# One fused attention and two-layer expert kernel: a new hand-written order for its first batch, and parts of the second batch's attention moved to later steps

## Chip, core and metric

The kernel runs on one core of one Trainium2 chip. The metric is the device time of one execution in microseconds (us). Of the kernel before, three runs are shown: 1402.45, 1406.14 and 1407.8 us, median 1406.14 us.

## What is computed

Three stages feed each other. Stage 1 is attention over a small memory: for each of 8 batches and 8 heads, `phi` (576 x 32) goes through a softmax and condenses `k` and `v` (576 x 64) into 32 memory rows; the queries attend to these 32 rows. Stage 2 takes the 4608 tokens with 512 features through two dense layers with an ELU between them. Stage 3 sends each token to one of 8 experts (the arg-max of a small product), through two more layers with a ReLU.

```python
a = softmax(phi); k_m = einsum('bhsm,bhsd->bhmd', a, k); v_m = einsum('bhsm,bhsd->bhmd', a, v)
x = softmax(q @ k_m.T / 8) @ v_m          # tokens x 512
g = elu(x @ w_in);  y = g @ w_out         # w_in 512 x 2048, w_out 2048 x 512, float64 in HBM
e = argmax(y @ w_gate);  out = gate * (relu(y @ w1[e]) @ w2[e])
```

## The kernel before

Stages 1 and 2 go batch by batch; the product of attention and the first layer is regrouped, so that a batch's `v_m` is first multiplied with `w_in` (names `M`, `n.M`) and the result, in `wt0`, is the stationary side of `mm1`. The unit of work is a step: `mm1` (6 matmuls, L509), `elu` (two ScalarE activations and one VectorE operation, L516 to L518), `split_g` (a ScalarE rounding L525 and a subtraction L526 on VectorE or GpSimd that gives high and low halves), `mm2` (12 matmuls, L541). A batch has 32 steps, two halves (g = 0, 1) of 16. Step numbers in this text count from the start: steps 0 to 31 are batch 0 (the half g = 1 is cut in two, so that its last 8 steps come at 24 to 31), step 32 is the first of batch 1. The matmuls of step i + 2 (`mm1`) are issued in loop turn i.

During the first batch the kernel also reads both weight matrices, which lie in HBM as 64-bit floats, and turns them into float32 halves by integer operations. For each of 16 loads n: `x.n` (DMA), `A0.n` (ScalarE, L264 and L269), `A1.n.r` (VectorE, L278, L281 and L284), `R.n.r` (GpSimd, L292). An even n is a slice of w_in, used by `M` and written to DRAM by `B.n`; an odd n is a slice of w_out, whose high half `C.n` (ScalarE, L308) makes and whose low half `D.n.r` (L320, 128 x 512) is made on VectorE where `LO_V` names (n, r), on TensorE where `LO_PE` does, else on GpSimd. `GL_V` likewise names the steps whose L526 is on VectorE. Slices 1, 6, 10 and 13 go in halves (r = 0, 1); for the others the names with r = 1 do nothing.

The attention of one batch comes in two halves u of four heads: `phi.u`, `kv.u`, `q.u` (loads), `a1`, `a1e` (softmax of phi), `a2` (transposes), `a3` (the sums over k and v, 48 records of L369, which wait for the kv load), `a3b`, `a4t`, `a4` (scores, L413), `a5`, `a5e`, `a5b`, `a5m` (softmax over 32), `a5c`, `a5d` (the operand of `mm1`, L458 on ScalarE and L459 on GpSimd). With `n.` in front they belong to batch 1. The kv tile has one buffer. In the first batch the same buffer holds the weight slices n >= 3 that are being converted (`conv_h`): they wait for `a3.1`, and the next `kv` load, `n.kv.0`, waits for the last of them.

The order of all this is written by hand: the string `START` is the order in which the named pieces are issued, and every engine and the DMA queue of SyncE works through its own share of it in that order. `LATER` puts further pieces in front of numbered loop turns from 23 on; from turn 24 on the framework orders instructions itself. Everything behind a waiting instruction on the same engine waits with it. `y_items` gives the turns, after a half-batch is finished, in which its tokens' expert is chosen, ranked and scattered.

```python
tag="kv"            # load_kv: one buffer, shared with conv_h["h"] for n >= 3
t = [1, 2, 4, 5, 6, 8, 10]   # y_items: logit, logit2, rank, first scatter, rows 0 to 2
```

Of the kernel before, what the change touches and what calls it, by code (L numbers as in the profile page):

```python
# [23 lines left out]


START = """
A1.5.1 phi.0 A1.12.1 kv.0 A1.9.1 a1.0 R.3.1 a1e.0 a2.0.0 phi.1 q.0 a2.0.1 routing x.3 a1.1 R.15.1 a1e.1 a3.0 a3b.0
a2.1.0 a4t.0 R.8.1 a2.1.1 kv.1 a4.0 a5.0 a3.1 x.2 R.0.1 A1.7.1 R.9.1 q.1 A0.3 A1.3.0 a5e.0 x.1 R.2.1 a5b.0 a5m.0
a3b.1 A0.2 a5c.0 R.11.1 R.3.0 a4t.1 x.0 A1.3.1 A1.2.0 a4.1 a5d.0 R.14.1 C.3 a5.1 A0.1 x.4 A1.1.0 R.2.0 A1.1.1 A0.0
a5e.1 D.3.1 A1.8.1 A1.0.0 A1.2.1 a5b.1 A0.4 R.7.1 A1.4.1 D.3.0 x.5 R.4.1 R.1.1 R.1.0 C.1 A1.4.0 R.0.0 a3c A0.5 a5m.1  # L30
a5c.1 D.1.0 A1.5.0 D.1.1 n.phi.0 R.4.0 a5d.1 M.0 R.5.1 Me.0 x.6 A0.6 M.1 B.0 n.a1.0 A1.6.0 B.4 Me.1 mm1.0 R.5.0 C.5
x.7 B.2 mm1.1 elu.0 M.2 elu.1 g.0 A1.11.1 mm1.2 x.8 mm1.3 A1.6.1 D.5.1 D.5.0 Me.2 g.1 R.6.0 elu.2 R.6.1 B.6 elu.3
A0.7 mm2.0 A1.7.0 g.2 x.9 g.3 mm2.1 M.3 mm1.4 A0.8 elu.4 mm1.5 mm2.2 Me.3 mm2.3 g.4 elu.5 R.7.0 A1.8.0 x.10 mm1.6
mm1.7 mm2.4 C.7 g.5 elu.6 elu.7 A0.9 D.7.0 n.phi.1 R.8.0 x.11 D.7.1 mm1.8 g.6 mm2.5 mm1.9 mm2.6 A1.9.0 R.12.1 g.7
elu.8 swap R.9.0 A1.15.1 mm2.7 A0.10 elu.9 mm1.10 g.8 part A1.10.0 A1.0.1 mm1.11 elu.10 elu.11 B.8 mm2.8 g.9 C.9
mm1.12 g.11 M.4 mm2.9 A1.10.1 mm1.13 D.9.1 g.10 elu.12 x.12 A0.11 mm1.14 D.9.0 mm2.10 A1.14.1 A1.11.0 mm2.11 Me.4
R.10.0 A0.12 elu.13 elu.14 g.13 R.10.1 R.11.0 g.12 M.5 A1.12.0 w.0 B.10 g.14 Me.5 mm1.15 mm1.16 mm2.12 C.11 R.12.0
x.13 elu.15 mm2.13 elu.16 D.11.1 A0.13 D.11.0 g.16 mm2.14 mm1.17 g.15 M.6 mm1.18 elu.17 A1.13.0 x.14 mm2.15 mm2.16
A0.14 A1.14.0 elu.18 x.15 mm1.19 g.17 Me.6 B.12 n.a1e.0 A1.13.1 g.18 A0.15 mm2.17 A1.15.0 mm1.20 n.a2.0 R.14.0 w.1
mm2.18 elu.19 M.7 elu.20 g.19 R.13.0 mm1.21 R.13.1 R.15.0 Me.7 g.20 mm2.19 B.14 C.13 D.13.0 D.13.1 elu.21 mm1.22  # L40
elu.22 g.21 C.15 g.22 n.a1.1 mm2.20 D.15.0 D.15.1 n.kv.0 n.q.1 n.a3.0 n.q.0 n.a1e.1 mm2.21 n.a3b.0 n.a4t.0 mm2.22
n.a2.1 n.a4t.1 n.a4.0 mm1.24 n.kv.1 n.a3.1 n.a5.0 mm1.23 elu.24 n.a3b.1 n.a5e.0 elu.23 g.24 g.23 n.a3c
"""
# [12 lines left out]

# [1226 lines left out]
```

## Time and profile before

| | |
|---|---|
| median of the three runs | 1406.14 us |
| the profiled execution | 1407.8 us |
| its span, first to last instruction | 1406.1 us |
| mean granted TensorE clock (1.00 is 2.4 GHz, 0.50 is 1.2 GHz) | 0.977 |
| busy: TensorE, its weight loads, VectorE, ScalarE, GpSimd | 93%, 80%, 44%, 45%, 31% |

PE is TensorE's matmuls, PEld its weight loads, DVE is VectorE, ACT is ScalarE, POOL is GpSimd, SP is SyncE, whose rows are DMA issues. A matmul's end is modelled, so neighbouring matmuls overlap in the rows; the distance of their starts is what one costs. In a timeline row the bracket is the idle time of the engine before the row and what ended it. The last letters of a matmul's name in the views are its operands: `ps_kv` is a3, `ps_s` a4, `ps_M` M, `ps_h` mm1, `ps_acc` mm2.

### The profile page before, as it was taken

The page shows a single profiled execution, that of the slowest core. Times are in us where ns is not written, and L with a number is a line of the kernel's source. Part 1 is how long each engine was busy: PE and PEld are TensorE (multiplying, and loading weights), DVE is VectorE, ACT ScalarE, POOL GpSimd, SP SyncE. Part 2 cuts the span into 40 slices and gives each one's busy share as a digit, 9 for nine tenths or more (in the row PEclk, how much of TensorE's full clock was granted, in tenths as well). Part 3 has the DMA queues.
Part 4 walks back from the last instruction along what each step waited for, and adds up shares of the span by engine and source line. Part 5 has one row for each costly group of instructions (what it writes and reads, how often), then busy time and mean ns, then how long its engine had stood idle before and what let it go on. Part 6 is the DMA issues. An engine that isn't in the chain of part 4 may idle for free. (4 is left out here: it accounts for less than half of the span.)

```text
span 1406.1 us, 27602 instructions
## 1 busy us (share of the span) xinstructions
PE 1304.9 (93%) x9407; PEld 1121.6 (80%) x9407; DVE 625.0 (44%) x1355; ACT 633.1 (45%) x1377; POOL 441.6 (31%) x480
## 2 busy tenths in 40 slices
PE   3498699999999999999899999999999999999996
PEld 2287588889889888799789889878888888888885
DVE  4998454343443534434433324553222555342221
ACT  3586255555565555555455556422111443231110
POOL 2665143334433433434334343221111111111111
PEclk9898799999999999999999999999999999999998
DMA  9765745235325333433421510054111444211110
GB/s 238 202 207 154 178 121 130 62 114 102 90 83 103 103 79 94 139 71 92 103 76 37 167 28 24 18 185 154 46 46 41 159 143 141 72 46 44 34 47 31
DMA packets 57626, 140.74 MB, mean 100 GB/s; under 512 B 9321, under 2 KB 21738, under 8 KB 53872
## 3 DMA queue, kind: packets, MB, share of 16 engines
q1 hardware_dynamic: 49328, 118.15, 30.5%
q0 software_dynamic: 8128, 20.50, 4.7%
q8 instruction: 85, 1.39, 0.5%
q14 instruction: 85, 0.70, 0.2%
HBM read 253.79 MB, written 24.02 MB: 198 GB/s over the span
## 5 line engine op out<-in xcount | busy, mean ns | idle before, releaser
L526 POOL TENSOR_TENSOR gl<-e,gh 128x288 fp32r<-128x288 f32 x243 | 198.7, 819 | 376.5 <-ACT gh L525 296.8
L541 PE MATMUL ps_acc<-gl,wt 128*128 128x288 f32 x1024 | 306.6, 299 | 6.3 <-DVE gl L526 3.6
L541 PE MATMUL ps_acc<-gh,wt 128*128 128x288 f32 x1024 | 305.7, 299 | 1.9 <-ACT gh L525 1.9
L541 PE MATMUL ps_acc<-gh,wol 128*128 128x288 f32 x1024 | 302.9, 296 | 0.0
L509 PE MATMUL ps_h<-ath,wt 128*128 128x288 f32 x1024 | 263.2, 313 | 10.0 <-DVE e L518 9.9
L509 PEld LDWEIGHTS ps_h<-ath,wt 128*128 128x128 f32 x1024 | 181.8, 192 | 50.2 <-issue 29.5
L518 DVE SCALAR_TENSOR_TENSOR e<-e,ps_h 128x288 f32<-128x288 f32 x256 | 114.7, 450 | 238.4 <-ACT e L517 201.8
L541 PEld LDWEIGHTS ps_acc<-gl,wt 128*128 128x128 f32 x1024 | 195.3, 191 | 12.5 <-DVE gl L526 6.4
L541 PEld LDWEIGHTS ps_acc<-gh,wt 128*128 128x128 f32 x1024 | 195.5, 191 | 2.9 <-ACT gh L525 2.5
L1109 PE MATMUL ps_h<-wt,xh 128*128 x592 | 196.2, 402 | 1.3 <-ACT xh L1090 0.8
L541 PEld LDWEIGHTS ps_acc<-gh,wol 128*128 128x128 f32 x1024 | 195.1, 191 | 0.0
L525 ACT CAST gh<-e 128x288 fp32r<-128x288 f32 x256 | 109.7, 430 | 153.0 <-DVE e L518 151.0
L1150 POOL DMA_INDIRECT out_dram<-ot,idw x37 | 37.1, 1004 | 390.4 <-DVE ot L1149 378.6
L509 PE MATMUL ps_h<-atl,wt 128*128 128x288 f32 x512 | 153.7, 300 | 0.0
L516 ACT ACTIVATE e<-ps_h 128x288 f32<-128x288 f32 x256 | 104.8, 410 | 82.3 <-PE ps_h L509 72.4
L1109 PEld LDWEIGHTS ps_h<-wt,xh 128*128 128x128 f32 x592 | 112.1, 189 | 27.2 <-ACT xh L1090 1.0
L1143 PE MATMUL ps_acc<-wt1h,hh 128*128 x296 | 120.9, 408 | 5.7 <-PEq L1187 5.7
L1125 ACT CAST hh<-ps_acc 128x512 fp32r<-128x512 f32 x74 | 39.8, 590 | 175.6 <-PE ps_acc L1123 175.5
L1143 PE MATMUL ps_acc<-wt1l,hh 128*128 x296 | 118.6, 401 | 0.0
L1109 PE MATMUL ps_h<-wt,xl 128*128 x296 | 117.9, 398 | 0.2 <-DVE xl L1091 0.2
L1143 PE MATMUL ps_acc<-wt1h,hl 128*128 x296 | 117.9, 398 | 0.0
L517 ACT ACTIVATE e<-e 128x288 f32<-128x288 f32 x256 | 113.8, 445 | 7.3
(242 smaller groups left out, 1829.3 us busy)
## 6 DMA issues: line engine op xcount, KB each, us to landing
raw<-in_moe_w_dram SPq DMA_DIRECT2D x78, 2048.0 KB
win<-win_s SPq DMA_DIRECT2D x28, 1024.0 KB
kv<-in_k_dram SPq DMA_DIRECT2D x16, 576.0 KB
kv<-in_v_dram SPq DMA_DIRECT2D x16, 576.0 KB
table<-yr SPq DMA_DIRECT2D x144, 64.0 KB
big<-in_moe_w_out_dram SPq DMA_DIRECT2D x10, 512.0 KB
phi_t<-in_phi_dram SPq DMA_DIRECT2D x16, 288.0 KB
big<-in_q_dram SPq DMA_DIRECT2D x16, 288.0 KB
```

What stands on the lines that cost most here:

```text
L509: nc.tensor.matmul(ps, x[:, u, fo:fo + P], y[:, u], start=(n == 0), stop=(n == 3 * NQ - 1))
L516: nc.scalar.activation(out=e, in_=ps, func=AF.Relu, scale=-1.0)
L517: nc.scalar.activation(out=e, in_=e, func=AF.Exp, scale=-1.0)
L518: nc.vector.scalar_tensor_tensor(out=e, in0=e, scalar=-1.0, in1=ps, op0=ALU.add, op1=ALU.max)
L525: nc.scalar.copy(out=gh, in_=e)
L526: eng.tensor_tensor(out=gl, in0=e, in1=gh.bitcast(F32), op=ALU.subtract)
L541: nc.tensor.matmul(acc[c], x[:, f, P * c:P * c + P], y, start=(first and n == 0), stop=(final and n == 2),)
L1109: nc.tensor.matmul(ps, x[:, c], half(wt[0][y][2 * c + hf]), start=(i == 0), stop=(i == 3 * NC - 1))
L1125: nc.scalar.copy(out=h, in_=ps)
L1143: nc.tensor.matmul(ps, get(h, f), half(wt[1][y][f]), start=(i == 0), stop=(i == 3 * NF2 - 1))
L1150: nc.gpsimd.indirect_dma_start(out=out, out_offset=IndirectOffsetOnAxis(ap=at, axis=0), in_=ot, in_offset=None, bounds_check=NT - 1, oob_i ...
```

## The change

Three things are replaced: the order of the first batch (`START`) and the two sets that place its subtractions; the turns in `LATER` of batch 1's attention; and the turns of the first half-batch's ranking. No operation is added or taken away. The two orders, their sets and the last line in full:

```diff
 START = """
-A1.5.1 phi.0 A1.12.1 kv.0 A1.9.1 a1.0 R.3.1 a1e.0 a2.0.0 phi.1 q.0 a2.0.1 routing x.3 a1.1 R.15.1 a1e.1 a3.0 a3b.0
-a2.1.0 a4t.0 R.8.1 a2.1.1 kv.1 a4.0 a5.0 a3.1 x.2 R.0.1 A1.7.1 R.9.1 q.1 A0.3 A1.3.0 a5e.0 x.1 R.2.1 a5b.0 a5m.0
-a3b.1 A0.2 a5c.0 R.11.1 R.3.0 a4t.1 x.0 A1.3.1 A1.2.0 a4.1 a5d.0 R.14.1 C.3 a5.1 A0.1 x.4 A1.1.0 R.2.0 A1.1.1 A0.0
-a5e.1 D.3.1 A1.8.1 A1.0.0 A1.2.1 a5b.1 A0.4 R.7.1 A1.4.1 D.3.0 x.5 R.4.1 R.1.1 R.1.0 C.1 A1.4.0 R.0.0 a3c A0.5 a5m.1
-a5c.1 D.1.0 A1.5.0 D.1.1 n.phi.0 R.4.0 a5d.1 M.0 R.5.1 Me.0 x.6 A0.6 M.1 B.0 n.a1.0 A1.6.0 B.4 Me.1 mm1.0 R.5.0 C.5
...
-mm2.18 elu.19 M.7 elu.20 g.19 R.13.0 mm1.21 R.13.1 R.15.0 Me.7 g.20 mm2.19 B.14 C.13 D.13.0 D.13.1 elu.21 mm1.22
-elu.22 g.21 C.15 g.22 n.a1.1 mm2.20 D.15.0 D.15.1 n.kv.0 n.q.1 n.a3.0 n.q.0 n.a1e.1 mm2.21 n.a3b.0 n.a4t.0 mm2.22
-n.a2.1 n.a4t.1 n.a4.0 mm1.24 n.kv.1 n.a3.1 n.a5.0 mm1.23 elu.24 n.a3b.1 n.a5e.0 elu.23 g.24 g.23 n.a3c
+routing phi.0 R.2.1 A1.9.1 x.1 kv.0 a1.0 A1.2.1 phi.1 a1e.0 A0.1 a2.0.0 R.7.1 a2.0.1 A1.1.0 A1.1.1 R.1.1 R.1.0 a3.0
+q.0 a1.1 a1e.1 a2.1.0 a3b.0 A1.8.1 R.5.1 a4t.0 x.2 kv.1 a2.1.1 A0.2 a4.0 C.1 q.1 a5.0 R.3.1 A1.7.1 x.3 A1.2.0 x.0
+a5e.0 a5b.0 D.1.1 D.1.0 a5m.0 a4t.1 a3.1 R.2.0 x.5 a5c.0 a3b.1 a4.1 a5d.0 A1.3.1 a5.1 A0.3 A1.3.0 a3c A0.0 a5e.1
+a5b.1 M.1 A1.0.0 R.3.0 R.0.1 A0.5 a5m.1 a5c.1 x.4 C.3 D.3.0 R.11.1 R.0.0 Me.1 A0.4 x.6 a5d.1 D.3.1 A1.4.0 B.2 M.0
+Me.0 R.4.1 A1.5.0 mm1.0 A0.6 elu.0 mm1.2 A1.6.0 R.14.1 elu.2 R.4.0 g.0 A1.4.1 M.2 Me.2 mm1.1 R.5.0 elu.1 R.12.1 C.5
...
+elu.18 g.16 A0.14 mm1.19 A1.14.0 R.13.1 mm2.16 g.18 elu.19 B.12 x.15 A0.15 n.q.0 mm1.20 A1.15.0 R.14.0 C.13 mm2.17
+mm2.18 g.19 w.0 elu.20 M.7 Me.7 mm1.21 elu.21 D.13.0 g.20 mm2.19 g.21 R.15.0 C.15 mm1.22 n.phi.1 D.13.1 mm2.20
+D.15.1 elu.22 D.15.0 B.14 mm2.21 g.22 n.q.1 n.kv.0 n.a4t.0 n.a1e.0 w.1 mm2.22 n.a2.0 n.a1.1 mm1.24 mm1.23 n.a4t.1
+elu.24 elu.23 g.24 g.23 n.a1e.1
 """
 LATER = {
-    23: "n.a5b.0 n.a5m.0 n.q2.0",
-    24: "n.M.0 n.a5c.0",
-    25: "n.pk2 n.a4.1 n.a5.1 n.a5e.1 n.a5b.1",
-    26: "n.q2.1",
-    27: "n.M.1",
-    29: "n.a5d.0",
-    30: "n.a5m.1 n.a5c.1 n.a5d.1",
-    31: "n.M.2",
-    35: "n.M.3",
+    24: "n.a3.0 n.a3b.0 n.kv.1 n.a2.1",
+    25: "n.a4.0 n.a5.0 n.a5e.0",
+    26: "n.a3.1 n.a3b.1 n.a5b.0 n.a5m.0 n.q2.0",
+    27: "n.pk2 n.a3c n.a4.1 n.a5.1 n.a5e.1 n.a5c.0",
+    28: "n.M.0 n.a5b.1 n.a5m.1 n.q2.1",
+    29: "n.a5d.0 n.a5c.1 n.a5d.1",
+    31: "n.M.1",
+    34: "n.M.2",
+    38: "n.M.3",
 }
-            LO_V = {(5, 0), (7, 1), (9, 1), (11, 0), (11, 1), (13, 0), (15, 0)}
+            LO_V = {(3, 0), (5, 1), (13, 1), (15, 0), (15, 1)}
-            GL_V = {0, 3, 4, 6, 12, 13, 14, 16, 18, 19, 21, 23, 24}
+            GL_V = {0, 1, 2, 4, 5, 6, 7, 8, 10, 11, 12, 14, 17, 19, 20, 21, 22, 23, 24}
-                t = [1, 2, 4, 5, 6, 8, 10] if g else [1, 2, 4, 5, 6, 8, 10]
+                t = [1, 2, 6, 7, 6, 8, 10] if b == 0 and g == 0 else [1, 2, 4, 5, 6, 8, 10]
```

## Rows read from the trace of the kernel before

**Rows 1.** Busy time by stretch: stretch, its length, PE, PEld, DVE, ACT, POOL, clock, DMA

```profile
0.00:200.00 200.00, 134.76 (x1110) 108.40 (x1111) 145.20 (x249) 107.87 (x211) 90.58 (x78) 0.88 0.69 185
200.00:400.00 200.00, 194.44 (x1756) 173.48 (x1754) 87.38 (x224) 112.69 (x265) 77.39 (x91) 1.00 0.41 105
```

**Rows 2.** The same view, in finer stretches of the first 198 us

```profile
0.00:26.00 26.00, 10.75 (x140) 7.58 (x140) 8.56 (x22) 6.24 (x11) 3.67 (x16) 1.00 0.93 230
26.00:62.00 36.00, 10.02 (x58) 3.79 (x58) 34.54 (x42) 21.58 (x32) 22.50 (x15) 0.95 0.76 201
62.00:125.00 63.00, 57.60 (x448) 50.32 (x448) 60.38 (x86) 51.73 (x103) 39.01 (x24) 0.95 0.73 214
125.00:141.00 16.00, 11.35 (x63) 9.61 (x63) 11.78 (x19) 7.68 (x17) 8.31 (x6) 0.66 0.29 98
141.00:150.00 9.00, 0.26 (x8) 0.29 (x12) 0.00 (x0) 0.06 (x2) 0.75 (x1) 0.50 0.86 200
150.00:198.00 48.00, 42.79 (x386) 34.81 (x379) 29.92 (x81) 19.29 (x46) 15.54 (x17) 0.81 0.50 141
```

**Rows 3.** Timeline of VectorE: start, duration, engine, line, operation, tiles

```profile
26.57 0.69 DVE L278 TENSOR_SCALAR conv_h<-conv_h 128x1024 f32<-128x1024 f32 x1 [5.86 <-ACT conv_h L264]
27.29 0.69 DVE L281 TENSOR_SCALAR conv_h<-conv_h 128x1024 uint32<-128x1024 uint32 x1
28.02 1.23 DVE L284 SCALAR_TENSOR_TENSOR conv_h<-big,conv_h 128x1024 uint32<-128x1024 uint32 x1
...
130.09 2.09 DVE L526 TENSOR_TENSOR gl<-e,gh 128x288 fp32r<-128x288 f32 x1
...
138.01 0.45 DVE L526 TENSOR_TENSOR gl<-e,gh 128x288 fp32r<-128x288 f32 x1
```

**Rows 4.** Timeline of GpSimd

```profile
20.89 1.16 POOL L428 TENSOR_TENSOR sT<-sT,mx 128x576 f32<-128x576 f32 x1 [17.46 <-DVE mx L423]
...
129.44 2.42 POOL L292 TENSOR_TENSOR conv_h<-conv_h,big 128x1024 uint32<-128x1024 uint32 x1 [2.76 <-DVE conv_h L284]
...
140.03 1.71 POOL L320 TENSOR_TENSOR wol<-conv_h,wt 128x512 fp32r<-128x512 f32 x1
...
185.23 1.55 POOL L459 TENSOR_TENSOR atl<-atT,ath 128x288 fp32r<-128x288 f32 x2 [0.59 <-ACT ath L458]
```

**Rows 5.** Groups by line, 0 to 152 us, VectorE: count, busy us, mean ns

```profile
L320 DVE TENSOR_TENSOR wol<-conv_h,wt 128x512 fp32r<-128x512 f32 x7 | 9.8, 1408 | 0.0
L526 DVE TENSOR_TENSOR gl<-e,gh 128x288 fp32r<-128x288 f32 x11 | 9.2, 844 | 0.2
```

**Rows 6.** The same view of GpSimd

```profile
L526 POOL TENSOR_TENSOR gl<-e,gh 128x288 fp32r<-128x288 f32 x12 | 12.2, 1022 | 14.6 <-ACT gh L525 14.6
L320 POOL TENSOR_TENSOR wol<-conv_h,wt 128x512 fp32r<-128x512 f32 x5 | 8.1, 1628 | 1.2 <-ACT wt L308 1.2
```

**Rows 7.** Timeline of TensorE

```profile
62.31 1.43 PE L471 MATMUL ps_M<-t,vT 64*32 64x256 f32 x16 [8.40 <-DVE wt L481]
63.67 0.61 PE L509 MATMUL ps_h<-ath,wt 128*128 128x288 f32 x1
...
149.74 2.79 PE L369 MATMUL ps_kv<-kv,a 96*32 96x128 f32 x48 [11.27 <-DMA kv<-in_v_dram]
...
160.00 1.52 PE L369 MATMUL ps_kv<-kv,a 96*32 96x128 f32 x48
...
197.94 0.30 PE L509 MATMUL ps_h<-ath,wt 128*128 128x288 f32 x1
198.08 0.30 PE L509 MATMUL ps_h<-atl,wt 128*128 128x288 f32 x1
```

**Rows 8.** Timeline of SyncE's DMA issues

```profile
141.78 0.34 SPq L196 DMA_DIRECT2D kv<-in_k_dram  x1
...
152.58 0.33 SPq L196 DMA_DIRECT2D kv<-in_k_dram  x1
```

**Rows 9.** Timeline of ScalarE

```profile
25.41 1.12 ACT L264 ACTIVATE conv_h<-big 128x1024 f32<-128x1024 f32 x1 [9.24 <-PE ps_kv L369]
```

More of the change, by code (lines that the diff above doesn't have):

```diff
@@ L32 @@
[L32 to L36, printed above, removed]
@@ L37 @@
-R.10.0 A0.12 elu.13 elu.14 g.13 R.10.1 R.11.0 g.12 M.5 A1.12.0 w.0 B.10 g.14 Me.5 mm1.15 mm1.16 mm2.12 C.11 R.12.0
-x.13 elu.15 mm2.13 elu.16 D.11.1 A0.13 D.11.0 g.16 mm2.14 mm1.17 g.15 M.6 mm1.18 elu.17 A1.13.0 x.14 mm2.15 mm2.16
-A0.14 A1.14.0 elu.18 x.15 mm1.19 g.17 Me.6 B.12 n.a1e.0 A1.13.1 g.18 A0.15 mm2.17 A1.15.0 mm1.20 n.a2.0 R.14.0 w.1
-mm2.18 elu.19 M.7 elu.20 g.19 R.13.0 mm1.21 R.13.1 R.15.0 Me.7 g.20 mm2.19 B.14 C.13 D.13.0 D.13.1 elu.21 mm1.22
-elu.22 g.21 C.15 g.22 n.a1.1 mm2.20 D.15.0 D.15.1 n.kv.0 n.q.1 n.a3.0 n.q.0 n.a1e.1 mm2.21 n.a3b.0 n.a4t.0 mm2.22
@@ new lines @@
+Me.0 R.4.1 A1.5.0 mm1.0 A0.6 elu.0 mm1.2 A1.6.0 R.14.1 elu.2 R.4.0 g.0 A1.4.1 M.2 Me.2 mm1.1 R.5.0 elu.1 R.12.1 C.5
+mm1.3 A1.6.1 B.4 elu.3 D.5.1 g.1 mm1.4 R.6.0 R.8.1 g.2 x.7 mm2.0 A0.7 A1.5.1 R.6.1 M.3 A1.7.0 elu.4 mm1.5 A1.15.1
+D.5.0 A1.14.1 x.8 mm2.1 x.9 mm2.2 g.3 Me.3 elu.5 mm1.6 mm1.7 B.6 mm2.3 R.7.0 A0.8 g.4 elu.6 A1.8.0 mm1.8 A1.12.1
+A1.11.1 elu.7 C.7 mm2.4 g.5 A0.9 mm1.9 g.7 g.6 A1.9.0 D.7.1 R.8.0 B.0 x.10 elu.8 D.7.0 B.8 A1.0.1 R.9.0 elu.9 A0.10
+mm2.5 g.8 swap R.9.1 mm2.6 n.phi.0 A1.10.0 mm1.10 mm2.7 M.4 elu.10 R.15.1 C.9 g.9 x.11 x.12 part mm1.11 elu.11
@@ new lines @@
+R.10.0 mm1.12 mm2.8 A1.10.1 Me.4 mm1.13 mm2.9 elu.12 g.10 A0.11 D.9.0 D.9.1 A1.11.0 mm1.15 R.10.1 x.13 mm2.10 elu.13
+M.5 mm1.14 g.11 g.12 mm2.11 A0.12 A1.12.0 mm2.12 R.11.0 g.13 B.10 mm2.13 elu.14 Me.5 elu.15 C.11 n.a1.0 g.14 R.12.0
+D.11.0 mm1.17 A0.13 D.11.1 M.6 mm1.16 elu.17 mm2.14 A1.13.0 x.14 mm1.18 g.15 elu.16 g.17 mm2.15 A1.13.1 R.13.0 Me.6
+elu.18 g.16 A0.14 mm1.19 A1.14.0 R.13.1 mm2.16 g.18 elu.19 B.12 x.15 A0.15 n.q.0 mm1.20 A1.15.0 R.14.0 C.13 mm2.17
+mm2.18 g.19 w.0 elu.20 M.7 Me.7 mm1.21 elu.21 D.13.0 g.20 mm2.19 g.21 R.15.0 C.15 mm1.22 n.phi.1 D.13.1 mm2.20
```

## The prediction, made before the changed kernel was run

> **What bounds the kernel now.** I began with busy time by stretch. From 200 us on TensorE is busy 194 of 200 us at a clock of 1.00 [rows 1]; no operation is added or removed, so that part can only start earlier or later. In the first 200 us TensorE is busy 135 us at a mean clock of 0.88. All that the change can give or cost lies here, up to the first matmul of step 32, the first of batch 1, which starts at 197.94 [rows 7].
>
> The finer stretches show three regimes [rows 2]. Until 26 us little runs: VectorE 8.6 us, GpSimd 3.7 us (2.5 of that is setup), while DMA is 93% busy. From 26 to 125 us VectorE is busy 94.9 of 99 us. Between 141 and 150 us nothing computes: TensorE waits 11.27 us for batch 1's kv load [rows 7]. The remainder to 198 us runs at a clock of 0.81, so TensorE is partly at its 1.2 GHz level after that idle time.
>
> VectorE's busy time holds waits. The same L526 takes 0.45 us alone, but 2.09 us when it begins while GpSimd is inside a 2.42 us L292 [rows 3, 4]: it ends only after it. Over the stretch its mean is 0.84 us on VectorE and 1.02 us on GpSimd [rows 5, 6]. The two take turns on operations that read two tiles in SBUF, so moving such work between them shortens little. What counts is when the pair gets its first weight slice. That was A0.3, held until 25.41 us because its output buffer was the kv buffer, released by a3.1 [rows 9].
>
> **Part 1, the first batch's order.** Slice 1 now loads ahead of kv.0 and converts in its own tile, not the kv buffer. SyncE meets routing's small write first, and that waits for a fill on GpSimd's queue; I put 2 us on the start. By DMA's 230 GB/s [rows 2] routing, phi.0 and slice 1 (1.5 MB) are in at about 11 us, kv.0 (1.15 MB) at about 15, against 149.74 - 141.78 = 8.0 us for a kv load by itself [rows 8, 7]. By 26 us VectorE then has done, beside setup and the same attention pieces, the two halves of slice 1 and slice 2. One whole slice costs 0.69 + 0.69 + 1.23 = 2.6 us [rows 3], the halves a little more, 3.1: some 5.7 us more, against a count of 6.3 when the attention pieces are laid out one by one. I take 6.
>
> Against that stands work moved onto VectorE before n.kv.0: six more L526 (steps up to 22: 17 now, 11 before), 6 x 0.84 = 5.1 us, and two L320 fewer, 2 x 1.41 = 2.8 us [rows 5]: VectorE gains 2.3 us of work. GpSimd loses 6 x 1.02 - 2 x 1.63 = 2.9 us [rows 6]. If VectorE alone is the limit, the conversion ends 6 - 2.3 = about 4 us earlier. If the turns are the limit, the pair has done by 26 us slice 1 on both engines (3.1 and 2 x 1.5), slice 2 on VectorE (2.6) and the 1.16 us of L428; only the last was there before: 8.7 us earlier, and the moved work is a wash. I take 7, nearer the second, since the long L526 show the turns. Call T the moment when n.kv.0 can be issued. It was 141.78 [rows 8], just after the last D.15 on GpSimd [rows 4]; it becomes 134.8, with ends 133 and 138. If the cover of the early loads is gone (kv.0 late makes u = 1 late), nothing of the 7 is left; that is a rival.
>
> **Part 2, batch 1's keys and values later.** Before, n.a3.0 stood in TensorE's queue behind mm2.20 and held mm2.21, mm2.22, both last mm1 of START and all later steps. Now ahead of it stand mm2.21 to mm2.23, mm1.23 to mm1.25 and n.a2.0. Neighbouring matmuls start 0.13 to 0.14 us apart [rows 7], so that is 54 x 0.132 = 7.1 us, and 0.8 for the six transposes: 7.9 us. kv.0 lands at T + 8.0. So the 11.27 us wait is covered but for hand-offs (elu.23 and g.23 must pass before mm2.23, about 2 us by three ScalarE and VectorE operations of 0.45): n.a3.0 starts at T + 10.
>
> What is then late is the chain behind it. kv.1 can be issued only when n.a3.0 has read the one buffer: T + 11.5. Before, from that issue (152.58) to n.a3.1 (160.00) took 7.4 us [rows 8, 7]: T + 19. TensorE has until then n.a2.1, two steps of 18 x 0.132 = 2.4, n.a4.0 and the first logits, about 8.4 us: T + 20. So n.a3.1 at T + 20.
>
> Here the new order puts w.1, 1 MB, into the queue behind kv.0 and so ahead of kv.1. The Trainium skill, *DMA: Bandwidth & Descriptors*, section Queues, rings and completion order, says that each DMA engine takes descriptors in ring order, which speaks against this place: kv.1 would first wait for what is left of that megabyte. By that rule, at the 200 GB/s of 141 to 150 us [rows 2], 5.2 us less the 3 since kv.0's landing are added, n.a3.1 moves by 1 us to T + 21, and the sum below would be 1390 in place of 1389.
>
> From n.a3.1 to the end of the last a5d (185.23 + 1.55 = 186.78) the chain took 26.8 us before [rows 7, 4]. Its own operations I estimate at 18 us: 1.5 for n.a3.1 and 1.6 for the L459 pair [rows 7, 4], a dozen between them at about 1 us (L428's 1.16 is a long one [rows 4]), and 0.2 us for each of 14 hand-offs. The rest was spent behind other work in the queues of VectorE, ScalarE and GpSimd. TensorE's work up to step 32 needs only some 14 us after n.a3.1 (five steps and the rest of attention), so this chain sets it: T + 38 to T + 47. I take T + 45, near the measured chain, because its neighbours in the queues are the same elu and split. Step 32 then starts at 134.8 + 45 = about 180, that is 18 us earlier. n.M.1 moves from before step 32 to behind it and gives back 1 us.
>
> **Part 3, the first ranks later.** The rank matmuls, scatters and the VectorE copies move by two turns. All stay inside TensorE-bound turns, and no one needs the ranks before the end of stage 2. Cost nothing; hidden by the 32 steps of batch 1. If it were not hidden, the rank's dozen small VectorE operations of about 0.2 us are 2.4 us at most. The later n.M.2 and n.M.3 still come ahead of the steps that use them.
>
> **Sum.** 7 (conversion) + 11 (kv wait and what follows) - 1 = 17 us. The profiled execution took 1407.8 us, 1.7 more than its span and 1.7 more than the median: 1390.8 on its scale, 1389 on the median's. The ends, T = 133 with T + 38 and T = 138 with T + 47, give 26 and 12 us: 1380 to 1394.
>
> **The rivals.**
> *The early gain is lost.* kv.0 behind slice 1 makes u = 1's scores late, mm1.0 starts no earlier than 63.67 [rows 7], T stays near 141.8. For it: DMA is 93% busy in that stretch [rows 2], and the load order is the only thing that moved. Against it: TensorE's last long wait ahead of mm1.0 (8.40 us) was for L481 in VectorE's queue, not for DMA [rows 7]. Then 10 us remain: 1396.
> *The kv wait only moves.* The chain from n.a3.0 to step 32 takes the 197.94 - 149.74 = 48.2 us it took before [rows 7], though less TensorE work lies in it, so that step 32 starts at T + 10 + 48.2 = 193: 5 us earlier, less 1: 1402. For it: the chain is longer than TensorE's work in either order.
> *Slower.* From turn 24 on the framework places the chain's 14 hand-offs among the steps, on VectorE, ScalarE and GpSimd alike. If each waits one whole step (2.4 us) in such a queue, step 32 comes at T + 38 + 34 = 207, 9 us later than before: 1415. It is slower from ten such waits on, by over 0.5% from thirteen; the 9 us of waits in the 26.8 us chain are four.
> *The change doesn't do what it says.* The new order fits the chip no better: T = 141.8 and the chain as before, step 32 at 200: 1408.
>
> **How the numbers follow.** Forecast 0.62, early gain lost 0.14, wait only moved 0.13, no better 0.06, slower 0.05. A measurement here can tell 0.5%, 7 us, from no change: faster means below 1399. That holds the forecast, the first rival and a third of the second: 0.81. Same: the rest of it and "no better", 0.14. Slower 0.05. The range reaches from 1379, just under the forecast's best end, to 1402, where the moved wait lies; the forecast alone is 1380 to 1394.
>
> **What would show it.** Right: the first slice's L278 near 12 us and not 26.57; mm1.0 at 50 to 57 us; the kv issue of batch 1 at 133 to 138; the wait before ps_kv under 3 us in place of 11.27, at the same n.a3.0; step 32 at 173 to 185; clock in the 48 us ahead of it over 0.81. Wrong: mm1.0 after 60, or a new wait of over 5 us on TensorE before step 32 (then look at who releases ps_kv's second half or ath); or different time behind 230 us, where I put nothing.

## The result, and the profile after

The changed kernel's median is 1390.84 us (four runs, 1389.06 to 1395.19) against 1406.88 us for the kernel before beside it (four runs): ratio 0.991, 95% interval 0.9885 to 0.9934. A second, later series, twelve runs against 22, gave 1396.04 against 1407.81 us: 0.9923 (0.9904 to 0.9943). The gain is 16.0 us in the first series and 11.8 in the second; I had forecast 17.

The profiled execution is the longest of the first four, 1395.19 us with a span of 1393.5 us, so its rows show 12.6 us of the gain: 1406.1 less 1393.5.

Busy time by stretch, changed kernel, same stretches and columns as [rows 1, 2]:

```profile
0.00:200.00 200.00, 140.78 (x1204) 111.88 (x1204) 150.88 (x268) 114.20 (x225) 85.90 (x78) 0.95 0.71 183
200.00:400.00 200.00, 195.03 (x1758) 173.25 (x1751) 87.18 (x218) 112.90 (x267) 77.28 (x92) 1.00 0.43 113
0.00:26.00 26.00, 7.96 (x92) 5.22 (x92) 10.88 (x27) 7.77 (x14) 5.02 (x17) 1.00 0.88 199
26.00:62.00 36.00, 18.58 (x142) 8.96 (x149) 27.97 (x41) 20.10 (x30) 18.30 (x12) 1.00 0.86 196
62.00:125.00 63.00, 52.18 (x396) 45.71 (x395) 60.65 (x82) 47.19 (x94) 35.11 (x23) 0.92 0.70 206
125.00:141.00 16.00, 11.84 (x95) 10.78 (x96) 15.86 (x22) 10.73 (x20) 8.36 (x5) 1.00 0.57 191
141.00:150.00 9.00, 3.92 (x31) 3.68 (x29) 5.84 (x12) 4.46 (x12) 0.00 (x0) 0.89 0.98 250
150.00:198.00 48.00, 44.29 (x436) 36.41 (x437) 29.11 (x88) 22.97 (x55) 18.78 (x21) 0.91 0.54 118
```

By 26 us VectorE has done 10.9 us of work in place of 8.6, not the 6 us more that I forecast; from 26 to 62 us it is busy 28.0 of 36 us, before 34.5: it now waits there. The hole from 141 to 150 us is half filled, and the clock of the last 48 us rose from 0.81 to 0.91.

Timeline of VectorE (first fence) and of ScalarE (second), changed kernel, the rows that end a wait for a load, and the first L278; [rows 3] has it at 26.57 us:

```profile
10.08 0.43 DVE L278 TENSOR_SCALAR t<-t 128x512 f32<-128x512 f32 x1 [1.71 <-ACT t L264]
...
18.02 0.78 DVE L336 STREAM_TRANSPOSE pT<-phi_t 128x576 f32<-128x576 f32 x1 [4.07 <-DMA phi_t<-in_phi_dram]
...
34.40 1.38 DVE L400 STREAM_TRANSPOSE big<-big 128x1152 f32<-128x1152 f32 x1 [2.32 <-DMA big<-in_q_dram]
```

```profile
26.42 1.13 ACT L264 ACTIVATE t<-win_x 128x1024 f32<-128x1024 f32 x1 [3.56 <-DMA win_x<-in_moe_w_in_dram]
...
39.28 1.12 ACT L264 ACTIVATE conv_h<-big 128x1024 f32<-128x1024 f32 x1 [2.04 <-DMA big<-in_moe_w_out_dram]
...
44.02 1.13 ACT L264 ACTIVATE t<-win_x 128x1024 f32<-128x1024 f32 x1 [2.47 <-DMA win_x<-in_moe_w_in_dram]
...
48.52 1.15 ACT L264 ACTIVATE conv_h<-win_x 128x1024 f32<-128x1024 f32 x1 [1.78 <-DMA win_x<-in_moe_w_out_dram]
```

Conversion starts 16.5 us earlier, and then the next four slices are each waited for: ScalarE stands 1.8 to 3.6 us for the load. Slice 2, which I had converted by 26 us, only lands then.

Timeline of TensorE, then of SyncE's issues, changed kernel, answering [rows 7] and [rows 8]:

```profile
17.10 2.79 PE L369 MATMUL ps_kv<-kv,a 96*32 96x128 f32 x48 [5.99 <-DMA kv<-in_v_dram]
...
59.95 0.40 PE L509 MATMUL ps_h<-ath,wt 128*128 128x288 f32 x1 [0.52 <-ACT wt L480]
...
150.64 0.60 PE L369 MATMUL ps_kv<-kv,a 96*32 96x128 f32 x2 [5.72 <-DMA kv<-in_v_dram]
...
155.88 1.29 PE L369 MATMUL ps_kv<-kv,a 96*32 96x128 f32 x38
...
165.83 1.52 PE L369 MATMUL ps_kv<-kv,a 96*32 96x128 f32 x48
...
185.79 0.29 PE L509 MATMUL ps_h<-ath,wt 128*128 128x288 f32 x1
```

```profile
140.49 0.33 SPq L196 DMA_DIRECT2D kv<-in_k_dram  x1
...
141.38 0.48 SPq L329 DMA_DIRECT2D win<-win_s  x1
...
157.22 0.33 SPq L196 DMA_DIRECT2D kv<-in_k_dram  x1
```

T is 140.49 (before 141.78). `n.a3.0` starts at T + 10.15 after a wait of 5.72 us for kv.0 (before 11.27), but its last 38 matmuls run only from 155.88: the framework dealt them out among `mm2.23` and `mm1.25`, so kv.1 was issued at T + 16.7. `n.a3.1` starts at T + 25.3, step 32 at 185.79 = T + 45.3, 12.1 us earlier than before.

### The profile page after: what moved, and what is told of

The parts are those of the page before. It is cut to its first block, busy times and chain, and to the rows that moved or that the text cites. A ratio compares the mean times of both kernels' runs of the same rounds, so it can differ in the third digit from the quotient of the medians.

```text
span 1393.5 us, 27587 instructions
## 1 busy us (share of the span) xinstructions
PE 1299.6 (93%) x9407; PEld 1114.5 (80%) x9407; DVE 626.4 (45%) x1359; ACT 633.6 (45%) x1377; POOL 433.9 (31%) x476
## 5 line engine op out<-in xcount | busy, mean ns | idle before, releaser
L526 POOL TENSOR_TENSOR gl<-e,gh 128x288 fp32r<-128x288 f32 x237 | 192.0, 812 | 382.2 <-ACT gh L525 296.7
L518 DVE SCALAR_TENSOR_TENSOR e<-e,ps_h 128x288 f32<-128x288 f32 x256 | 115.1, 450 | 230.1 <-ACT e L517 200.7
```

What stands on the lines that cost most here:

```text
L518: nc.vector.scalar_tensor_tensor(out=e, in0=e, scalar=-1.0, in1=ps, op0=ALU.add, op1=ALU.max)
```

## The experiments

Twelve kernels ran in three groups of four; a group shares a chip and its runs of the kernel before, which the ratio is taken against. e1 to e8 ran on one chip, e9 to e12 on another; which chip the first two traces are from isn't recorded. The table gives, for every trace, us from the start of the span: the issue of n.kv.0 (T), the start of n.a3.0, the issue of n.kv.1, the start of n.a3.1, the first `mm1` of steps 32 and 64, and the distances of steps 32 to 64 and 64 to 80. The last columns are medians of runs and the ratio with its interval. Line numbers in an experiment's rows can lie one or two lower or higher, where its `START` takes another number of lines.

| kernel | T | a3.0 | kv.1 | a3.1 | 32 | 64 | 32-64 | 64-80 | median, runs | ratio |
|---|---|---|---|---|---|---|---|---|---|---|
| before | 141.8 | 149.7 | 152.6 | 160.0 | 197.9 | 301.3 | 103.4 | 48.9 | 1406.88, 4 | |
| changed | 140.5 | 150.6 | 157.2 | 165.8 | 185.8 | 290.6 | 104.8 | 48.9 | 1390.84, 4 | 0.991 |
| e1 later alone | 141.3 | 149.0 | 151.8 | 169.7 | 189.6 | 300.7 | 111.1 | 52.5 | 1408.91, 10 | 1.0018 (0.9999-1.0037) |
| e2 order alone | 136.5 | 144.4 | 147.3 | 155.9 | 194.7 | 300.5 | 105.8 | 52.3 | 1405.55, 10 | 0.9991 (0.9972-1.0009) |
| e3 old ranks | 137.7 | 146.7 | 153.7 | 162.2 | 183.6 | 292.2 | 108.6 | 52.5 | 1400.27, 8 | 0.9962 (0.9944-0.998) |
| e4 extra load | 140.8 | 151.0 | 157.8 | 166.4 | 186.3 | 291.9 | 105.6 | 52.0 | 1399.27, 1 | |
| e5 changed again | 137.7 | 148.0 | 154.4 | 163.0 | 183.0 | 287.4 | 104.5 | 52.6 | 1396.04, 12 | 0.9923 (0.9904-0.9943) |
| e6 old sets | 143.8 | 154.6 | 156.1 | 164.8 | 184.7 | 289.5 | 104.8 | 51.9 | 1399.19, 7 | 0.9944 (0.9924-0.9963) |
| e7 kv, turn 23 | 140.5 | 150.3 | 152.1 | 161.6 | 181.5 | 287.0 | 105.5 | 52.3 | 1396.75, 4 | 0.9929 (0.9904-0.9954) |
| e8 w.1 moved | 137.2 | 147.9 | 149.4 | 158.1 | 178.1 | 283.0 | 104.9 | 52.7 | 1393.31, 6 | 0.9911 (0.9882-0.994) |
| e9 before again | 140.9 | 148.9 | 151.7 | 158.8 | 193.1 | 297.8 | 104.7 | 52.2 | 1406.48, 1 | |
| e10 later and ranks | 140.8 | 148.6 | 151.4 | 169.0 | 190.3 | 294.6 | 104.3 | 52.0 | 1403.33, 10 | 0.9969 (0.9954-0.9984) |
| e11 routing later | 135.5 | 145.4 | 152.6 | 161.2 | 179.6 | 285.7 | 106.0 | 54.5 | 1395.99, 4 | 0.9918 (0.9888-0.9948) |
| e12 three moves | 136.0 | 145.8 | 148.5 | 157.9 | 176.4 | 282.3 | 105.9 | 54.4 | 1389.84, 6 | 0.9874 (0.9848-0.9899) |

**Each part by itself (e1, e2).** e1 is the kernel before with batch 1's attention moved as in the change, but with its own order, sets and ranks:

```diff
-mm2.20 D.15.0 D.15.1 n.kv.0 n.q.1 n.a3.0 n.q.0 n.a1e.1 mm2.21 n.a3b.0 n.a4t.0 mm2.22
-n.a2.1 n.a4t.1 n.a4.0 mm1.24 n.kv.1 n.a3.1 n.a5.0 mm1.23 elu.24 n.a3b.1 n.a5e.0 elu.23 g.24 g.23 n.a3c
+mm2.20 D.15.0 D.15.1 n.kv.0 n.q.1 n.q.0 n.a1e.1 mm2.21 n.a4t.0 mm2.22 n.a4t.1 mm1.24 mm1.23 elu.24 elu.23 g.24 g.23
-    23: "n.a5b.0 n.a5m.0 n.q2.0",
+    24: "n.a3.0 n.a3b.0 n.kv.1 n.a2.1",
...
```

> The old order of the first batch and the old sets, with n.a3, n.a3b, n.a2.1, n.a4.0, n.a5.0, n.a5e.0, n.kv.1 and n.a3c taken out of it and placed as the change places them in LATER; the old turns of the ranks. Theory A (the whole gain comes from moving batch 1's work): T, the issue of batch 1's first kv load, stays at 141 to 143 us, step 32 starts at T + 45, 186 to 189 us, and the run is 10 to 14 us faster than before (ratio 0.990 to 0.993). Theory B (the new early order is needed for it, because the old order ends the weight conversion with idle time that the moved work would only lengthen): step 32 not before 193 us and the ratio 0.996 or above.

e2 is the reverse: the changed kernel's order up to the last conversion and its two sets, with the old end of the order, the old later turns and the old ranks:

```diff
-mm2.21 g.22 n.q.1 n.kv.0 n.a4t.0 n.a1e.0 w.1 mm2.22 n.a2.0 n.a1.1 mm1.24 mm1.23 n.a4t.1 elu.24 elu.23 g.24 g.23 n.a1e.1
+g.22 n.q.1 n.kv.0 n.a1e.0 n.a2.0 n.a3.0 n.a1.1 n.a1e.1 mm2.21 n.a3b.0 n.a4t.0 w.1 mm2.22 n.a2.1 n.a4t.1 n.a4.0 mm1.24 n.kv.1 n.a3.1 ...
-    24: "n.a3.0 n.a3b.0 n.kv.1 n.a2.1",
+    23: "n.a5b.0 n.a5m.0 n.q2.0",
...
```

> The new order of the first batch and the new sets up to the last conversion, then batch 1's work in the order of before, the old LATER and the old turns of the ranks. Theory A: T at 140 to 141 us as in the changed kernel, but TensorE then waits 8 to 11 us for n.a3.0 and step 32 comes about 56 us after T, at 195 to 198; ratio 0.998 to 1.001. Theory B: the new order carries a part of the gain, step 32 at or before 192 and the ratio 0.996 or less.

Neither is worth anything that a measurement can tell: 1.0018 and 0.9991, and both intervals hold 1. In e1 step 32 comes at 189.6 us, 3.5 us earlier than in the second trace of the kernel before (e9, on the other chip), but steps 32 to 64 then take 111.1 us. The timeline of TensorE in e1 names two new waits of 6.7 us together:

```profile
186.76 0.64 PE L653 MATMUL ps_y<-ident,ysb 128*96 128x128 f32 x4 [2.72 <-DVE wt L480]
...
200.52 1.09 PE L653 MATMUL ps_y<-ident,ysb 128*96 128x128 f32 x4 [3.96 <-DVE wt L480]
```

`ps_y` shares its PSUM tiles with `ps_M`, and waits for VectorE to empty one (L481, here L480): VectorE is late. In e2 T is 4.4 us earlier than in e9, yet step 32 is not: 194.7 against 193.1 us; what the order won was spent mostly in the chain from n.a3.1 on, 38.8 us against 34.3.

**The first ranks (e3, e10).** e3 is the changed kernel with the old turns of the first ranks, e10 is e1 with the new ones:

```diff
-                t = [1, 2, 6, 7, 6, 8, 10] if b == 0 and g == 0 else [1, 2, 4, 5, 6, 8, 10]
+                t = [1, 2, 4, 5, 6, 8, 10] if g else [1, 2, 4, 5, 6, 8, 10]
```

> The changed kernel with the old turns of the first half-batch's ranks (rank at the 4th turn behind it and not the 6th). Theory A (the turns of the ranks are hidden): T unchanged, step 32 within 2 us of 185.8, ratio to before as the changed kernel's within 0.002. Theory B (the ranks stand in the way of the attention chain on VectorE): step 32 3 us later or more, with a wait on TensorE before ps_r of over 3 us.

> The kernel before with batch 1's keys and values moved to the later turns and with the later turns for the first ranks, but with its own first order and sets. With the later turns of batch 1's attention alone, step 32 came 8 us earlier, and then steps 32 to 64 took 111.1 us against 103.4 before, so that nothing was left: 1.0018. Theory (the first half-batch's rank, at its old turns, stands in VectorE's queue among the moved attention): with the ranks later, steps 32 to 64 take 104 to 106 us, the whole is 4 to 6 us shorter than the kernel before, 0.996 to 0.997. Rival (the ranks cost nothing wherever they stand, as I predicted; the 111 us come from the old order's leftovers): steps 32 to 64 stay near 110 us, ratio 1.00.

This line was to cost and bring nothing. With it e1's 1.0018 becomes 0.9969 in e10, and steps 32 to 64 take 104.3 us in place of 111.1; without it the changed kernel's 0.9923 becomes 0.9962 in e3, and they take 108.6 in place of 104.5. Both pairs of intervals are disjoint (the second by a hair). By the ratios it is worth (1.0018 - 0.9969) x 1407 = 6.9 us and (0.9962 - 0.9923) x 1407 = 5.5 us; the bare medians of e3 and e5, on one chip, lie 4.2 us apart. Neither theory for e3 held: step 32 is not late, and yet the time is longer. How, the rows show, one trace of each. First e3, timelines of several engines, ten rows in order of time:

```profile
175.05 1.11 POOL L665 DMA_INDIRECT itab<-ids,di  x1 [0.33 <-DVE r_pos L637]
...
175.50 1.89 DVE L640 SCALAR_TENSOR_TENSOR rowb<-ecap,less 128x8 f32<-128x8 f32 x1
...
176.19 1.17 POOL L441 TENSOR_TENSOR sT<-sT,sm 128x576 f32<-128x576 f32 x1
...
177.32 1.36 DVE L400 STREAM_TRANSPOSE big<-big 128x1152 f32<-128x1152 f32 x1
...
180.15 0.75 DVE L446 STREAM_TRANSPOSE atT<-sT 128x576 f32<-128x576 f32 x1
...
184.30 0.78 DVE L336 STREAM_TRANSPOSE pT<-phi_t 128x576 f32<-128x576 f32 x1 [0.52 <-POOL atl L459]
...
185.10 6.46 SPq L190 DMA_DIRECT2D phi_t<-in_phi_dram  x2
...
190.41 0.78 DVE L336 STREAM_TRANSPOSE pT<-phi_t 128x576 f32<-128x576 f32 x1 [1.65 <-DMA phi_t<-in_phi_dram]
...
191.89 1.28 DVE L481 TENSOR_TENSOR wt<-ps_M,wt 128x512 fp32r<-128x512 f32 x2
...
192.63 1.07 PE L654 MATMUL ps_y<-ident,ysb 128*96 128x128 f32 x4 [2.22 <-DVE wt L481]
```

The same of e5, the changed kernel on the same chip (its L640 and its scatter, L665, come later, after the L336, and its L400 after the L446):

```profile
175.37 1.16 POOL L441 TENSOR_TENSOR sT<-sT,sm 128x576 f32<-128x576 f32 x1 [0.41 <-DVE sm L436]
...
176.56 0.78 DVE L446 STREAM_TRANSPOSE atT<-sT 128x576 f32<-128x576 f32 x1 [1.27 <-POOL sT L441]
...
180.33 0.77 DVE L336 STREAM_TRANSPOSE pT<-phi_t 128x576 f32<-128x576 f32 x1
...
181.32 7.45 SPq L190 DMA_DIRECT2D phi_t<-in_phi_dram  x2
...
185.53 0.15 DVE L640 SCALAR_TENSOR_TENSOR rowb<-ecap,less 128x8 f32<-128x8 f32 x1
...
187.63 0.77 DVE L336 STREAM_TRANSPOSE pT<-phi_t 128x576 f32<-128x576 f32 x1
...
189.17 1.29 DVE L481 TENSOR_TENSOR wt<-ps_M,wt 128x512 fp32r<-128x512 f32 x2
...
189.92 0.64 PE L654 MATMUL ps_y<-ident,ysb 128*96 128x128 f32 x4
```

Read down. Until the end of L436, which ends at 175.2 us in e3 and at 175.3 in e5, the two run level: so far the rank's small operations in VectorE's queue have cost the chain nothing. Then three things come together. GpSimd is in the rank's first scatter (L665), so L441 is 0.8 us late. VectorE is in the rank's L640, which takes 1.89 us in place of 0.15 and ends with L441 at 177.4. And L400, L481 and L518, 2.8 us in all, stand ahead of the second half's L446, where in e5 they come behind it. So L446 is 3.6 us late. Behind it batch 2's first L336, released by L459 on GpSimd, is 4.0 us late; only when it has read its `phi` tile is the next `phi` load issued, 3.8 us late; the second L336 then waits 1.65 us for that load, the L481 behind it is 2.7 us late, and TensorE waits 2.22 us for the PSUM tile. With the ranks two turns later that row has no wait. In e3 step 32 itself is not late (T + 45.9 against T + 45.2): the price falls due behind it. The rows account for this one wait; the rest of the 4.1 us between steps 32 and 64 was not followed.

**The changed kernel again, and the kernel before again (e5, e9).** Both unaltered. The reason was the column 64-80: the first two traces have 48.9 us both, e1 to e4 have 52.0 to 52.5, and that looked like a cost of the parts.

> The changed kernel once more, unaltered, beside the parts on one chip. So far either part alone was level with the kernel before (1.0018 and 0.9991), and the change with the old rank turns gave 0.9962, against 0.991 for the whole. Theory (the orders are worth it only together): the whole stays at 0.991, 1392 to 1396 us in all its runs, and its steps 64 to 80 take 48.9 us again as in its first profile, where the parts took 52.3. Rival (the condition of the run): its first four runs lay well; here it comes out at 0.994 to 0.997, about 1400 us and level with the run with the old rank turns, and steps 64 to 80 take 52 us in it too, so that this stretch is no matter of the first ranks' turns.

> The kernel before, unaltered, for its trace on the chip on which the parts ran. The changed kernel's second trace took 52.6 us for steps 64 to 80, its first 48.8, the first trace of the kernel before 48.9. Theory (the condition of the run): steps 64 to 80 take 52 to 53 us here too, though none of the change's parts is in it, and the distance of the two kernels' step 64, not that of their ends, is what the parts are compared by. Rival (the new orders make that stretch longer): 48.9 us as in its first trace.

It is none: the kernel before has 52.2 us there too, though its trace came from the other chip and not, as was meant, from that of the parts. In all twelve later traces, on two chips, the stretch takes 51.9 to 54.5. So the theory for e5 fell on its mark, and its runs reach from 1394.1 to 1405.2 us, not 1392 to 1396; the rival held on that stretch but not on e3: the whole beats the run with the old ranks. The first series lay 5 us better than the second in the changed kernel and 1 us better in the kernel before; why, is open.

**What paces the first 60 us (e4, e11).** e4 adds an unused 1 MB load behind slice 1's, ahead of kv.0; e11 moves the routing table's write, which waits for a fill on GpSimd, from the front of the order back to where it was:

```diff
                 conv_x[n] = t.rearrange("p r (n t) -> p r n t", t=2)
+                if n == 1:
+                    y = pool.tile([P, 2, 1024], U32, tag="win", name="win_y", bufs=2)
+                    for r in range(2):
+                        nc.sync.dma_start(out=y[:, r], in_=w_out[P * r:P * r + P, :])
```

```diff
-routing phi.0 R.2.1 A1.9.1 x.1 kv.0 a1.0 A1.2.1 phi.1 a1e.0 A0.1 a2.0.0 R.7.1 a2.0.1 A1.1.0
+phi.0 R.2.1 A1.9.1 x.1 kv.0 a1.0 A1.2.1 phi.1 a1e.0 A0.1 a2.0.0 R.7.1 a2.0.1 routing A1.1.0
```

> The changed kernel with one more load of 1 MB right behind slice 1's, into a buffer that nothing reads. Theory A (in the new order the loads pace the first 55 us): each later wait for a load ends about 1.05 MB / 0.22 MB per us = 4.8 us later; the first matmul of mm1 starts at 63 to 65 us in place of 59.95. Theory B (VectorE and GpSimd pace it as before): the first mm1 moves by under 2 us, since the 8 us that VectorE idles between 26 and 62 us take the delay. In both, T moves by less than the first mm1, because the pair of engines has idle time to fill.

> The changed kernel with the routing table's write moved from the front of the order back to where it stood before, behind a2.0.1. In its trace this write is issued at 3.47 us, behind a fill on GpSimd, and holds phi.0, slice 1 and kv.0 behind it: the first kv issue is at 5.3 us, before it was at 2.6. Theory (DMA paces the first 55 us): all loads come 1.5 to 2.7 us earlier, the first slice's L278 at 8 us, mm1.0 and T 2 us earlier, the time 2 us shorter, 0.9985 of the changed kernel's. Rival (VectorE and GpSimd pace it from 26 us on): the first L278 comes earlier, T stays within 1 us, and the time too.

mm1.0 is at 59.95 and 58.03 us in the two traces of the changed kernel, 55.6, 57.1, 61.0 and 57.4 in e2, e3, e7 and e8, which alter nothing ahead of it. e4's 59.93 lies inside that spread, and its T of 140.8 just above theirs (136.5 to 140.5): the 4.8 us of theory A don't show, and nothing follows from it alone. In e11 the first kv issue is at 3.55 us in place of 5.3, mm1.0 at 54.80 and T at 135.5, in e12 with the same move 55.32 and 136.0: below the spread, but by 1 us or less. What the spread itself follows says more. In all nine traces with the new sets (the two of the changed kernel, e2 to e4, e7, e8, e11 and e12) ScalarE's L264 of slice 2 ends a wait for its load. It starts between 21.76 us (e11) and 27.18 (e4), and mm1.0 comes 32.3 to 33.9 us and T 112.5 to 114.1 us behind it. The load's own time varies: in the first 26 us DMA moved 199 GB/s in the first trace of the changed kernel, 211 in e5, 219 in e2. So across these traces mm1.0 and T follow the loads almost us for us, and the 1.7 us at the front of their queue go with a T that is 2.6 us earlier (135.8, the mean of two traces, against 138.4, that of six). The end doesn't show it: ratio 0.9918 beside 0.9923.

**The sets (e6).** The changed kernel with the old `LO_V` and `GL_V`:

```diff
-            LO_V = {(3, 0), (5, 1), (13, 1), (15, 0), (15, 1)}
+            LO_V = {(5, 0), (7, 1), (9, 1), (11, 0), (11, 1), (13, 0), (15, 0)}
-            GL_V = {0, 1, 2, 4, 5, 6, 7, 8, 10, 11, 12, 14, 17, 19, 20, 21, 22, 23, 24}
+            GL_V = {0, 3, 4, 6, 12, 13, 14, 16, 18, 19, 21, 23, 24}
```

> The changed kernel with the two sets of the kernel before that place L320 and L526 on VectorE or GpSimd. Theory (the two engines take turns, so placing is a wash): T within 2 us of the changed kernel's beside it, the time within 0.2%. Rival (VectorE alone is the limit): six L526 fewer and two L320 more before T take 2.3 us from VectorE, so T comes 2 us earlier; or the new order was found with these sets in mind, and a subtraction on the other engine is late where the order expects it: T comes 3 us later or more, the time 0.2 to 0.4% longer.

T comes at 143.8, 3.3 us later than any of the six traces with the new sets and that start (136.5 to 140.5), and 118.1 us behind slice 2's L264, where the nine have 112.5 to 114.1; mm1.0, at 56.7, is early. So in this one trace the placing isn't a wash at T: the old sets cost 4 us or more. By step 32 it has shrunk to 1.8 us against e5, since n.a3.0 here runs in one piece; the ratios, 0.9944 and 0.9923, overlap.

**The kv chain (e7, e8, e12).**

```diff
-    24: "n.a3.0 n.a3b.0 n.kv.1 n.a2.1",
+    23: "n.a3.0 n.a3b.0 n.kv.1",
+    24: "n.a2.1",
```

> The changed kernel with n.a3.0, n.a3b.0 and n.kv.1 in front of turn 23 instead of 24, so that the framework no longer deals the 48 matmuls of n.a3.0 out among mm1.25 and mm2.23. In the changed kernel's profile they ran from 150.64 to 157.1 us and kv.1 was issued at 157.22. Theory (the one kv buffer sets the chain): n.a3.0 takes 3 us in one piece, kv.1 is issued at about T + 13 in place of T + 16.7, n.a3.1 starts at T + 21 to T + 22 in place of T + 25.3, step 32 at T + 41 to T + 43 in place of T + 45.3, the time 3 us shorter. Rival (the queues of VectorE and ScalarE set the chain behind n.a3.1): step 32 stays at T + 45, and as the wait for kv now holds mm1.25 and mm2.23 too, the time is the same or up to 3 us longer.

```diff
-D.15.1 elu.22 D.15.0 B.14 mm2.21 g.22 n.q.1 n.kv.0 n.a4t.0 n.a1e.0 w.1 mm2.22
+D.15.1 elu.22 D.15.0 B.14 mm2.21 g.22 n.q.1 n.kv.0 n.a4t.0 n.a1e.0 mm2.22
-    24: "n.a3.0 n.a3b.0 n.kv.1 n.a2.1",
+    24: "n.a3.0 n.a3b.0 n.kv.1 w.1 n.a2.1",
```

> The changed kernel with w.1, 1 MB, issued behind n.kv.1 instead of right behind n.kv.0. In the changed kernel's profile n.a3.0 started 10.15 us after the issue of kv.0, where a kv load by itself took 8.0 before. Theory (the megabyte shares the DMA engines with kv.0, whose last packets then come late): n.a3.0 starts at T + 8 to T + 8.5, the wait ahead of it falls from 5.7 to under 4 us, and the time is 1 to 2 us shorter. Rival (the queue is taken in order, so what is issued behind kv.0 can't delay it): n.a3.0 stays at T + 10, and only kv.1 gains; the time stays within 1 us.

e7 did what it says: n.a3.0 in one piece, kv.1 at T + 11.6, n.a3.1 at T + 21.1, step 32 at T + 41.0. The time is the same within the interval; its T happened to be 2.8 us later than e5's, so step 32 is only 1.5 us earlier. e8 did not do what it says. The framework, which orders from turn 24 on, drew the load of w.1 ahead, as SyncE's row and TensorE's show:

```profile
135.29 0.42 SPq L328 DMA_DIRECT2D win<-win_s  x1
...
137.19 0.33 SPq L195 DMA_DIRECT2D kv<-in_k_dram  x1
...
147.87 1.52 PE L368 MATMUL ps_kv<-kv,a 96*32 96x128 f32 x48 [0.17 <-DMA kv<-in_v_dram]
```

The megabyte stands ahead of kv.0 here, and kv.0 lands 10.7 us after its issue, so neither theory was tried. e2 speaks against the first: there too w.1 is issued 0.9 us behind kv.0, and n.a3.0 starts at T + 7.9. But n.a3.0 now comes in one piece behind the work that it was mixed with, so step 32 stands at T + 40.9. Again the 4 us are those of the undivided n.a3.0: in the five traces of the new order and later turns where it is divided, step 32 stands at T + 44.2 to T + 45.9, in the four where it isn't (e6, e7, e8, e12) at T + 40.3 to T + 41.0.

> The changed kernel with three moves together: the routing write behind a2.0.1, n.a3.0, n.a3b.0 and n.kv.1 in front of turn 23, and w.1 behind n.kv.1. Alone, the second gave step 32 at T + 41.0 and the third at T + 40.9, in place of T + 45.3, and the times 1396.75 and 1393.31 beside 1396.04 us of the changed kernel. Theory (T and the chain behind it are separate terms): T 2 us earlier than beside it, step 32 at T + 38 to T + 41, together 6 us at step 32 and 4 to 6 us at the end: 1390 to 1392 us on this chip, 0.988 of the kernel before. Rival (the later steps wait for something else, the rank or batch 2's loads): step 32 comes 6 us earlier, the end no more than 2 us.

e12, in turn 23 by hand, did place w.1 behind kv.1:

```profile
136.05 0.33 SPq L196 DMA_DIRECT2D kv<-in_k_dram  x1
...
148.46 0.31 SPq L196 DMA_DIRECT2D kv<-in_k_dram  x1
...
149.35 0.47 SPq L329 DMA_DIRECT2D win<-win_s  x1
```

Step 32 at 176.4 us is T + 40.3, 6.6 us earlier than e5's; by step 64 5.1 us of it are left, by step 80 3.3. At the end the median is 1389.84 us, ratio 0.9874 (0.9848 to 0.9899), disjoint from the changed kernel's 0.9923: 6 to 7 us faster (by the bare medians, on two chips, and by the ratios), and the best version of the study.

## Why the prediction was right, and where it wasn't

The time came out at 1390.84 us where 1389 was forecast, and at 1396.04 in the second series, inside the range but 2 us past the forecast's own 1380 to 1394. The sum was right; its terms were not. Of the six signs of being right that I had named two came: the first L278 at 10.08 us and the clock of 0.91. mm1.0 (59.95 us for 50 to 57), the kv issue (140.49 for 133 to 138), the wait (5.72 for under 3) and step 32 (185.79 for 173 to 185) did not. So that the first series came within 2 us of the forecast was luck: step 32 moved by 12.1 us where I had 18, and the profiled execution (12.6 us) and the second series (11.8) lie at the low end of my 12 to 26.

**Part 1, T.** Failed step: the 7 us by which T was to come earlier. It was mis-sized: 1.3 us in the first trace, and in the six traces with this start and these sets T lies at 136.5 to 140.5 us, in the four with the old start (before, e1, e9, e10) at 140.8 to 141.8. The first L278 came at 10.08 us (said: near 12), but "by 26 us VectorE then has done the two halves of slice 1 and slice 2" took loads for granted. kv.0 kept a3.0 waiting until 17.10 us, where I had it in at 15 (my own rate of 230 GB/s gives 16), and slice 2 landed at 26. DMA was the first thing that I read as busy there, 93% [rows 2], and I then counted engine work only; what T followed was slice 2's load (e4, e11). The price of the moved work was low as well. Groups by line, 0 to 152 us, VectorE, answering [rows 5]:

```profile
L526 DVE TENSOR_TENSOR gl<-e,gh 128x288 fp32r<-128x288 f32 x19 | 20.0, 1075 | 1.2 <-ACT gh L525 1.0
...
L320 DVE TENSOR_TENSOR wol<-conv_h,wt 128x512 fp32r<-128x512 f32 x5 | 6.2, 1251 | 0.0
```

One L526 costs 1.08 us in place of the 0.84 that I multiplied with. Up to T the 17 L526 take 19.1 us (before 11 take 9.2) and the five L320 6.2 (before seven take 9.8): VectorE gained 6.3 us of work where I had 2.3, and T was still earlier than with the old sets (e6). More of them beside GpSimd's L292 means longer ones: the row's mean is no price for moving more of the same onto that engine. The Trainium skill, *SBUF — State Buffer*, section Who interferes with whom, says that VectorE and GpSimd share one pair of ports as an exclusive lock, that a VectorE instruction with two inputs in SBUF contends there with a GpSimd one that reads SBUF, and that the order of issue decides which of the two is blocked. The long L526 of [rows 3] behind the L292 of [rows 4] agrees. So does the changed kernel's trace: an L526 that starts at 134.66 us, 0.16 us ahead of an L292, takes 0.45 us, and one that starts at 94.06, 1.25 us behind an L292, takes 1.50. L640 in e3 ends with L441 too; as GpSimd went into L441 from a scatter that had begun 0.45 us ahead of L640, the rows don't show which of the two held it.

**Part 2, the chain.** T + 10 for n.a3.0 came out (10.15, and 10.2 in e5), but not for my reason. I had kv.0 landing at T + 8.0 and TensorE busy with other work up to T + 10; TensorE was idle from T + 4.4, and the load landed at T + 10.15. In e2 it landed at T + 7.9; why it takes 2 us longer here is open. So the wait of "under 3 us" was 5.72: the load was late, and mm2.23 and mm1.25, which I had placed ahead of n.a3.0, came among its matmuls. Failed step: "kv.1 can be issued at T + 11.5": it was T + 16.7, and n.a3.1 came at T + 25.3 in place of T + 20. The next leg made up for it: from n.a3.1 to step 32 took 20.0 us where I had 25. So T + 45 was right (45.3) by two errors of 5 us; e7, without the first, has T + 41. The rule that I took from the Trainium skill, *DMA: Bandwidth & Descriptors*, section Queues, rings and completion order, and by which the sum would have been 1390, found nothing to act on: w.1 was issued 15.8 us ahead of kv.1.

**Part 3, the ranks.** Failed step: "Cost nothing; hidden by the 32 steps of batch 1." I asked what the rank costs at its new turns, 2.4 us at most, and not what it costs at its old ones, once batch 1's attention has been moved there. It is 5.5 to 6.9 us, about half of the gain. And I priced VectorE's operations only: in e3 the scatter on GpSimd and the order behind it make L446 late.

**The rivals.** "The kv wait only moves" has e1's time, 1.0018, but not its mechanism: from n.a3.0 to step 32 e1 takes 40.7 us, not the 48.2 of before, and loses what it won behind step 32 (111.1 us). In the changed kernel that leg is 35.2 us. "The early gain is lost" holds for most of T, not for the whole: from e10 to e5 the order with its sets and its end gives (0.9969 - 0.9923) x 1407 = 6.5 us; at step 32 the two traces, from two chips, are 7.3 us apart, 3.1 of it at T and the rest in the leg from T to step 32, 45.2 against 49.5 us. "Slower" came nowhere near with the three together. The terms of the sum don't add: order alone 1.3 us, later turns alone -2.5, both 5.3; later turns and ranks 4.4; all three 10.8 (the first two are not clear of noise). The ranks alone, and the order with the ranks, were not run.

Open: against e5, e11 is 2.3 us ahead at T and 3.3 at step 32, and level at step 80; e12 is 6.6 us ahead at step 32 and 3.3 at step 80 (64-80 takes 54.5 and 54.4 us). Both traces come from the other chip and from runs above their kernel's median (1401.35 against 1395.99, 1395.54 against 1389.84 us); how much of the loss that explains is not shown.

## What to carry to other kernels

Price a moved step also by what it makes of the work that already stands at its new place: a dozen operations of 0.2 us and a scatter are cheap by their own time, and dear when a reload that waits for its buffer and a shared PSUM tile stand behind them in the same queues. When a change has several parts, run them in pairs as well as singly: here two parts of three are worth nothing alone, and the third was not tried alone. And an engine that starts earlier meets the loads next, so count bytes along with busy time.
